# A retention layer fused with a low-rank mixer and an MLP: decay kept inside 64-token chunks instead of on the queries, and the attention steps moved within each tile

## The chip, the core and the metric

The kernel runs on one NeuronCore of a Trainium2 chip. A core has TensorE (PE in the profile, with its weight loads shown apart as PEld), VectorE (DVE), ScalarE (ACT), GpSimd (POOL) and SyncE (SP), each with its own instruction queue, and 16 DMA engines that all queues share. Matrix products land in PSUM; DVE and ACT bring them to SBUF. The metric is the device time of one execution in microseconds (us); lower is better.

## The reference

Eight batches, eight heads, 576 tokens, head width 64, model width 512, MLP width 2048, mixer rank 32:

```python
scores = scale * np.matmul(q, k.transpose(0, 1, 3, 2))
gamma = 1.0 - 2.0 ** (-5.0 - np.arange(H, dtype=np.float32))
Dmat = np.where(rel >= 0, gamma[:, None, None] ** rel[None, :, :], 0.0)   # rel = query - key
ret = scores * Dmat[None, :, :, :]
attn = np.matmul(ret, v)                     # (8, 8, 576, 64), then heads side by side: x (8, 576, 512)
h = xt @ U @ V                               # along the tokens, rank 32
u = x + h.transpose(0, 2, 1)
out = u + np.maximum(u @ w_ch1, 0.0) @ w_ch2
```

There is no softmax, so a query's result is a sum over keys with weights gamma^(query - key). That can be split in chunks of 64 tokens: inside a chunk the scores are computed and masked; everything from earlier chunks comes through one 64x64 state per chunk, the running sum of (key outer value).

## The kernel before

**Tiles and batches.** The MLP works in nine tiles of 512 tokens, which run over the batch borders (a batch has 576). A tile is 32 units on TensorE: units 0 to 15 make the 16 slices of the hidden layer (four accumulating matmuls, then a ReLU on ACT that copies PSUM to SBUF, `y1`), units 16 to 31 make the four output blocks, four units each (then an addition on DVE, `o_sb`, and a store on SP's queue). One unit is four matmuls of 512 columns, some 0.86 us in the trace. Tiles are numbered j = 0 to 8. Batches 0 and 1 and tile 0 are done by `early`, whose order is written out by hand (the string `EARLY`). Then tile j carries the attention of batch j + 1, for j = 1 to 6; tiles 7 and 8 carry none. Where a batch's tokens begin inside a tile, a unit's matmuls are split by columns.

**Steps.** `attention_steps(b, at, gap, at_mixer, at_turn)` lists pieces of a batch's attention with a time in units, and the last loop of the kernel emits, before unit n, every step whose time is at most n. Every engine works through its own instructions in the order emitted. A batch has four head pairs (hp). For each, `att_transposes` at `at[hp]` brings q and k in the layout that TensorE wants, and `visit` at `at[hp] + gap` does the work; a fifth visit at `at[4]` finishes the last pair. For batch 2, q and k are turned on TensorE into PSUM (`psq`, `psk`); ACT copies k (`kvT`) and DVE takes q. From batch 3 on both are turned by DMA transposes (SP's queue) one tile ahead, into `qT_all`/`kT_all` or, every other batch, `qz`/`kvT`.

**One visit.** `visit(b, n)` emits, in this order: the state products of the pair before (`chunk_values`: `xh<-S,q`, 16 matmuls of 64 columns, each waiting for its own slice of `S`); this pair's state terms (`chunk_states`: `pss<-k,v`, 16 to 18 matmuls, and on ACT the copy of the first state to `S`); this pair's scores (`chunk_scores`: `sc<-q,k`, 20 matmuls); the masked scores times v for the pair before (`block_values`: `xh<-v,ret`, 10 matmuls, and on ACT the two copies `x_t<-xh`). Then on DVE: the two masks (`ret<-sc,mask`) and the chain of seven additions `S[g] = pss[g] + S[g-1]`.

**Where the decay is.** gamma^(query - key) is written as gamma^query times gamma^-key over the whole batch. `scale_q_dense` multiplies q by `qsrow` (gamma^token, one row per head) on DVE: 12 head pairs' `qT_all` and 8 pairs' `qz` in place, in bf16, and batch 2's four straight from PSUM. The values are multiplied by gamma^-token times 1/8 (`vscales[2]`): for batch 2 by DVE (`scale_v`, one step per pair, one unit before its transposes), from batch 3 on by POOL, block by block, between its load instructions (`scale_block`). The mask is then 0 or 1 and the same for all heads (`mask64`), and the states only add up.

**Buffers.** PSUM: three banks `mm` shared by the MLP's units and the two `xh` of a visit; three `att` for scores, transposes and the mixer; one double bank for `pss`. The mixer (`mix_middle` at `at_mixer`, five `mix_up` from `at_mixer + 2` half a unit apart, then DMA transposes of `u_t` into `uT_t` from `at_mixer + 3.2`) ends a batch. POOL waits for these transposes before it loads the batch three further on (`wait_for_turns`). In tile 1 the first three units are already done by `early`, and the mixer steps of batch 1 (`late`, at units 14, 20, 24.2, 27, 26 and 29) stand among batch 2's.

Of the kernel before, what the change touches and what calls it, by code (L numbers as in the profile page):

```python
# [8 lines left out]
FP32 = mybir.dt.float32  # L9
BF16 = mybir.dt.bfloat16  # L10
# [53 lines left out]
def kernel(  # L64
# [110 lines left out]
    iota_pc = consts.tile([P, NB], FP32, name="iota_pc")  # L175
    landed = consts.tile([P, NB], BF16, name="landed")
    lnbias = consts.tile([P, 1], FP32, name="lnbias")
    mask64 = consts.tile([P, 2, CH], BF16, name="mask64")
    lngam = consts.tile([P, NHP], FP32, name="lngam")
    qsrow = consts.tile([P, NHP, SP], BF16, name="qsrow")  # L180
    vscales = [consts.tile([P, H, NB], FP32, name=f"vscale{i}") for i in range(NFULL + 1)]
    vexp = consts.tile([P, H, NB], FP32, name="vexp")
    shifted = consts.tile([P, NFULL], FP32, name="shifted")
    masklast = consts.tile([P, 3 * CH], BF16, name="masklast")
    U_sb = [consts.tile([P, NB, P], BF16, name=f"U_sb{i}") for i in range(2)]
    V_sb = [consts.tile([P, SP], BF16, name=f"V_sb{i}") for i in range(2)]
# [55 lines left out]
    def by_head(x):  # L242
        return x.rearrange("p h c -> p c h")[:, :, :, None].to_broadcast([P, NB, H, D])

    vs_b = by_head(vscales[NFULL])

    def scale_v(b, hp):
        v_all = v_sets[b % NSET]
# [60 lines left out]
    def scale_q_runs(b, hp, psq):  # L309

        qT = qz_bufs[hp % 2][:, 0, :]
        c = slice(0, S) if b % 2 == 0 else slice(SP - S, SP)
        dve.tensor_tensor(
            out=by_token(qT[:, c]), in0=psq.rearrange("d i p -> d p i"),
            in1=by_token(qsrow[:, hp, c]), op=ALU.mult,
        )
        return qT

    def att_transposes(b, hp, st):
        if b < NRUNS:  # L320
            psq = turn_runs_by_head(in_runs(q_raw[b % NRUNS]), hp, "psq")
        elif b < NTURN:
            psq = turn_blocks(in_blocks(q_raw[b % NRUNS]), hp, "psq")
        else:
            psq = qT_sets[(b - NTURN) % 2][:, :, hp, :]
        st["qT"] = scale_q_dense(b, hp, psq)
        if b < NTURN:
            psk = turn_blocks(k_sets[b % NSET], hp, "psk")
            st["kT"] = kT_bufs[hp % 2].rearrange("p (c i) -> p c i", c=NB)
            act.copy(out=st["kT"], in_=psk)  # L330
        else:
            st["kT"] = kT_sets[(b - NTURN) % 2][:, :, hp, :]


    def scale_q_dense(b, hp, psq):
        if b >= NTURN:
            dve.tensor_tensor(
                out=psq, in0=psq, in1=qsrow[:, hp, :].rearrange("d (c i) -> d c i", c=NB),
                op=ALU.mult,
            )  # L340
            return [psq[:, g // 2, half(g)] for g in range(NS)]
        qT = scale_q_runs(b, hp, psq)
        return [qT[:, g * CH:(g + 1) * CH] for g in range(NS)]

    def chunk_states(b, hp, st):

        k_all, v_all = (x[b % NSET] for x in (k_sets, v_sets))
        ps = banks["two"].tile([P, 2, 8, CH], FP32, tag="pss", name="pss64")
        gs = places(b)[:-1]
        for g in gs:  # L350
            for hl in range(2):
                h = 2 * hp + hl
                pe.matmul(
                    ps[half(hl), g % 2, g // 2, :], k_all[half(g), g // 2, h, :],
                    v_all[half(g), g // 2, h, :], start=True, stop=True, skip_group_check=True,
                )
        S_sb = work.tile([P, NS - 1, CH], BF16, tag="S_sb", name="S64")
        st["S"] = S_sb
        act.copy(out=S_sb[:, gs[0], :], in_=ps[:, gs[0] % 2, gs[0] // 2, :])

        def add_up():
            for g in gs[1:]:
                dve.tensor_tensor(
                    out=S_sb[:, g, :], in0=ps[:, g % 2, g // 2, :], in1=S_sb[:, g - 1, :],
                    op=ALU.add,
                )

        return add_up

    def chunk_scores(st):  # L370


        sc = [banks["one"].tile([P, 8, CH], FP32, tag="att", name="sc64") for _ in range(2)]
        for g in range(NS):
            for hl in range(2):
                pe.matmul(
                    sc[hl][half(g), g // 2, :], st["kT"][half(hl), g // 2, half(g)],
                    st["qT"][g][half(hl), :], start=True, stop=True,
                    skip_group_check=True,
                )  # L380
        st["ret"] = work.tile([P, 2, NB, P], BF16, tag="ret", name="ret64")

        def mask():
            for hl in range(2):
                dve.tensor_tensor(
                    out=st["ret"][:, hl, :, :].rearrange("p c (i t) -> p c i t", i=2),
                    in0=sc[hl][:, 0:NB, None, :].to_broadcast([P, NB, 2, CH]),
                    in1=mask64[:, None, :, :].to_broadcast([P, NB, 2, CH]), op=ALU.mult,
                )

        return mask
# [13 lines left out]
    def block_values(b, hp, st, xs, x_t):  # L405
        for hl in range(2):
            h = 2 * hp + hl
            for m in range(NB):
                pe.matmul(
                    xs[hl][:, m, :], st["ret"][:, hl, m, :], v_sets[b % NSET][:, m, h, :],  # L410
                    start=False, stop=True, skip_group_check=True,
                )
            act.copy(out=x_t[:, :, h * D:(h + 1) * D], in_=xs[hl][:, 0:NB, :])

    def visit(b, n, sts, x_t):

        if n > 0:
            xs = chunk_values(b, sts[n - 1])
        if n < NHP:
            add_up = chunk_states(b, n, sts[n])  # L420
            mask = chunk_scores(sts[n])
        if n > 0:
            block_values(b, n - 1, sts[n - 1], xs, x_t)
        if n < NHP:
            mask()
            add_up()
# [450 lines left out]
    def exp_of(x):  # L877
        act.activation(out=x, in_=x, func=AF.Exp, bias=lnbias, scale=1.0)
# [66 lines left out]
    for b, x in enumerate(vscales):  # L945
        dve.tensor_tensor(out=x, in0=vexp, in1=places_of, op=ALU.mult)
        if b < NFULL:
            c = ((NB - 1), 0)[b]
            moved = shifted[:, b:b + 1]
            dve.tensor_scalar(  # L950
                out=moved, in0=iota_pc[:, c:c + 1], scalar1=float((-HALF, HALF)[b]),
                scalar2=None, op0=ALU.add,
            )
            dve.tensor_tensor(
                out=x.rearrange("p (g i) c -> p g i c", i=2)[:, :, 1 - b, c],
                in0=vexp.rearrange("p (g i) c -> p g i c", i=2)[:, :, 1 - b, c],
                in1=moved.to_broadcast([P, NHP]), op=ALU.mult,
            )
        if b == 0:
            exp_of(x)  # L960

    dve.memset(U_sb[0], 0.0)
    dve.memset(V_sb[0], 0.0)
# [31 lines left out]
    def between():  # L995

        dve.memset(k_sets[0][HALF:P, NB - 1, :, :], 0.0)
        for i in range(2):
            dve.memset(k_sets[1][half(1 - i), 0, i::2, :], 0.0)
        dve.memset(pairs[0]["u"][HALF:P, NB - 1, :], 0.0)  # L1000
        for x in (k_sets, v_sets):
            dve.memset(x[2][HALF:P, NB - 1, :, :], 0.0)
        dve.memset(q_raw[1][NR:P, :], 0.0)
        for x in at_diag:
            dve.memset(x, 0.0)
        dve.tensor_copy(out=mask64.rearrange("p i t -> p (i t)"), in_=maskbin)
        dve.memset(mask64[0:CH, 1, :], 0.0)

    units1, steps1 = mlp_units(1)
    late = early(mlp_units(0)[1], steps1, between)  # L1010
    for x in (k_sets, v_sets):
        dve.memset(x[3][0:HALF, 0, :, :], 0.0)
    load_batch(3)
# [5 lines left out]
    for j in range(1, NT):  # L1019
        if j == 1:  # L1020
            load_batch(4, range(3))
        steps = []
        if j == 1:
            steps = sorted(
                attention_steps(2, (0, 4.5, 9, 13, 19), 1.5, 20.5, 8) + late,
                key=lambda s: s[:2]
            )
        elif j + 1 < B:
            steps = attention_steps(j + 1, (-1, 3, 7, 11, 17), 1.5, 18.5)
        for n, unit in enumerate(units1 if j == 1 else mlp_units(j)[0]):  # L1030
            while steps and steps[0][0] <= n:
                steps.pop(0)[2]()
            if j > 1 or n >= 3:
                unit()
        for s in steps:
            s[2]()

        if j + 4 < B:
            wait_for_turns(j + 1)
            if j == 1:  # L1040
                load_batch(4, range(3, NB))
            load_batch(j + 4)
# [30 lines left out]
```

## Time and profile before

| | |
|---|---|
| median of 3 runs | 344.21 us (342.31 to 344.47) |
| the profiled execution | 344.57 us |
| its span, first to last instruction | 342.1 us |
| PE busy | 323.0 us, 94% |
| DVE busy | 178.8 us, 52% |
| ACT busy | 143.5 us, 42% |
| POOL busy | 129.2 us, 38% |
| mean granted TensorE clock | 0.995 |

The span is the time between the first and the last instruction; 2.5 us of the execution lie around it. Busy time counts the instructions of an engine; matmuls overlap, and their ends are modelled. In a group or a timeline, "out<-in" names what an instruction writes and reads, "x7" how many are merged, and what stands in brackets is the idle time in front and what ended it. "issue" means that the engine waited for nothing that the profile shows. All instructions carry line 25, a helper through which every operation is made, so groups are told apart by the tiles they write and read.

### The profile page before, as it was taken

What the parts mean: (1) busy time and instruction counts of PE and PEld (TensorE: products, weight loads), DVE (VectorE), ACT (ScalarE), POOL (GpSimd) and SP (SyncE); (2) the same over time, 40 slices, a digit from 0 to 9 for tenths busy, and PEclk for the clock granted to TensorE, in tenths of its full rate; (3) what the DMA queues carried; (4) which work ended last, traced back from release to release, by engine and by line L of the source; (5) the groups of instructions that cost most, each with busy time, mean ns of one, the idle gap of its engine ahead of it and who ended that gap; (6) DMA issues with size and microseconds to landing.
All of it is one profiled execution on the core that took longest, in us unless ns stands there. A gap on an engine that the chain in (4) does not pass through costs nothing.

```text
span 342.1 us, 8895 instructions
## 1 busy us (share of the span) xinstructions
PE 323.0 (94%) x3771; PEld 176.1 (51%) x3800; DVE 178.8 (52%) x432; ACT 143.5 (42%) x304; POOL 129.2 (38%) x166
## 2 busy tenths in 40 slices
PE   7989999979998899898999799999999999999994
PEld 3764455645545664454458654454467544444441
DVE  5866276578775865376437625674477430020011
ACT  7766532557412661076206430474057306504600
POOL 8942784999108991694079420000000000000000
PEclk9999999999999999999999989999999999999999
DMA  8999999999949999999999977640500050011011
GB/s 134 190 207 205 184 201 200 140 147 141 129 108 132 134 163 164 141 161 131 112 133 155 142 65 149 151 59 20 135 34 5 31 140 31 0 63 61 0 61 62
DMA packets 145112, 39.49 MB, mean 115 GB/s; under 512 B 132400, under 2 KB 140336, under 8 KB 145072
## 3 DMA queue, kind: packets, MB, share of 16 engines
q0 software_dynamic: 92848, 17.77, 64.7%
q1 hardware_dynamic: 52224, 21.16, 32.5%
q8 instruction: 29, 0.48, 0.6%
q14 instruction: 11, 0.09, 0.1%
HBM read 37.14 MB, written 9.44 MB: 136 GB/s over the span
## 4 chain that ended last, share of the span: by engine, by line
PE 84%; DVE 6%; DMA 4%; issue 3%; ACT 0%; POOL 0%; DVEq 0%; POOLq 0%
PE ps_y L25 67%; PE ps_b L25 6%; PE xh L25 4%; DMA kv_runs<-in_v_dram 3%; PE sc L25 2%; PE ps_h L25 2%; DVE ret L25 2%; DVE qT_all L25 2%; DMA q_all<-in_q_dram 2%; DVE S L25 1%; DVE v_all L25 1%; DVE qz L25 1%; PE ps_at L25 1%; PE pss L25 1%; PE psk L25 0%
## 5 line engine op out<-in xcount | busy, mean ns | idle before, releaser
L25 ACT ACTIVATE y_t<-ps_y 128x512 bf16<-128x512 f32 x144 | 85.6, 597 | 123.1 <-PE ps_y L25 122.9
L25 PE MATMUL ps_y<-uT_t,w_sb 128*128 128x512 bf16 (+3 forms) x768 | 134.0, 329 | 0.8 <-issue 0.8
L25 PE MATMUL ps_y<-w_sb,y_t 128*128 128x512 bf16 x549 | 129.6, 379 | 2.2 <-issue 1.3
L25 PEld LDWEIGHTS <-w_sb 128*128 128x128 bf16 x768 | 68.9, 99 | 52.4 <-issue 1.1
L25 PEld LDWEIGHTS <-y_t 128*128 128x128 bf16 x576 | 54.9, 98 | 63.4 <-issue 0.3
L25 DVE TENSOR_TENSOR o_sb<-ps_y,u_t 128x512 f32<-128x512 f32 x36 | 24.9, 690 | 107.0 <-PE ps_y L25 107.0
L25 DVE TENSOR_TENSOR ret<-sc,mask 128x640 bf16<-128x640 f32 x48 | 37.3, 819 | 17.4 <-PE sc L25 15.2
L25 DVE TENSOR_TENSOR S<-pss,S 128x64 bf16<-128x64 f32 x168 | 37.4, 223 | 4.9
L25 POOL DMA_DIRECT2D q_all<-in_q_dram x37 | 30.1, 817 | 6.0 <-DMA w_sb<-in_moe_w_ch_dram 3.7
L25 POOL DMA_DIRECT2D k_all<-in_k_dram x30 | 24.4, 816 | 12.4 <-DMA w_sb<-in_moe_w_ch_dram 8.9
L25 DVE TENSOR_TENSOR u_t<-ps_h,x_t 128x512 bf16<-128x512 f32 (+1 forms) x35 | 22.7, 685 | 4.6 <-PE ps_h L25 4.4
L25 ACT CAST x_t<-xh 128x320 bf16<-128x320 f32 x48 | 18.1, 429 | 12.5 <-PE xh L25 11.1
L25 POOL TENSOR_TENSOR v_all<-v_all,vscale 128x512 bf16<-128x512 bf16 (+1 forms) x15 | 16.7, 1116 | 3.9 <-DMA v_all<-in_v_dram 3.9
L25 POOL DMA_DIRECT2D v_all<-in_v_dram x20 | 17.2, 859 | 1.6 <-issue 0.9
L25 POOL COPY landed<-uT_t 128x4 bf16<-128x4 bf16 (+1 forms) x3 | 0.6, 184 | 38.6 <-DMA uT_t<-u_t 38.6
L25 POOL TENSOR_TENSOR kv_runs<-kv_runs,vscale 128x512 bf16<-128x512 bf16 (+1 forms) x10 | 10.7, 1069 | 9.0 <-DMA kv_runs<-in_v_dram 8.8
L25 PEld LDWEIGHTS <-ret 128*128 128x128 bf16 (+1 forms) x320 | 11.6, 98 | 2.9 <-DVE ret L25 0.8
L25 PEld LDWEIGHTS <-kvT 64*64 64x64 bf16 (+3 forms) x360 | 8.4, 103 | 7.0 <-issue 3.9
L25 POOL DMA_DIRECT2D kv_runs<-in_k_dram x14 | 11.3, 804 | 1.3 <-POOLq L1057 0.9
L25 PEld LDWEIGHTS <-k_all 64*64 64x64 bf16 (+2 forms) x456 | 9.2, 109 | 4.5 <-issue 3.1
L25 POOL DMA_DIRECT2D kv_runs<-in_v_dram x14 | 11.1, 793 | 0.2 <-issue 0.2
L25 ACT CAST at_diag<-ps_at 32x128 bf16<-32x128 f32 x24 | 6.2, 257 | 9.6 <-PE ps_at L25 9.4
(104 smaller groups left out, 241.2 us busy)
## 6 DMA issues: line engine op xcount, KB each, us to landing
out_dram<-o_sb SPq DMA_DIRECT2D x36, 256.0 KB, 2.1
w_sb<-in_moe_w_ch_dram POOLq DMA_DIRECT2D x8, 512.0 KB, 11.8
q_all<-in_q_dram POOLq DMA_DIRECT2D x20, 128.0 KB, 7.4
k_all<-in_k_dram POOLq DMA_DIRECT2D x16, 128.0 KB, 9.1
v_all<-in_v_dram POOLq DMA_DIRECT2D x16, 128.0 KB, 9.5
q_all<-in_q_dram POOLq DMA_DIRECT2D x12, 144.0 KB, 6.8
kv_runs<-in_v_dram SPq DMA_DIRECT2D x8, 128.0 KB, 6.3
kv_runs<-in_k_dram POOLq DMA_DIRECT2D x8, 128.0 KB, 7.5
```

Source lines behind the costliest of these rows:

```text
L25: return self._tc.keep_in_program_order(call(*args, **kwargs))
```

## The change

Only batches 2 to 7 are touched. gamma^(query - key) is now counted from the start of each 64-token chunk, in four places, with p the place of a token in its chunk:

- **Queries are not scaled.** From batch 3 on nothing is done to q. For batch 2, `q_by_chunks` copies it from PSUM on ACT.
- **The values** are multiplied by 1/8 times gamma^(64 - p): `vs64`, by the same instructions as before (DVE for batch 2, POOL later), with another table.
- **The masks** take a power and are one per head, in fp32 (`masks`, 8 x 128 x 128, laid over `qsrow`, which `early` has done with). DVE makes them with eight `tensor_scalar` between `early` and tile 1.
- **The copies** `x_t<-xh` on ACT become activations with a per-partition factor (`xs64`).
- **The states** decay by gamma^64 from chunk to chunk: the seven additions become `scalar_tensor_tensor`, S[g] = S[g-1] * keep64 + pss[g], with a per-partition scalar.

Seven tiny set-up instructions come in on DVE and ACT and two go out. The step times change: batch 2's pairs from (0, 4.5, 9, 13, 19) and mixer 20.5 to (3, 7, 11, 15, 20.5) and 22; batches 3 to 7 from (-1, 3, 7, 11, 17) and 18.5 to (-1.5, 2.5, 6.5, 10.5, 16) and 17.8. With the gap of 1.5 the visits of batches 3 to 7 come before units 0, 4, 8, 12 and 16 (were 1, 5, 9, 13, 17), the mixer before unit 18 (was 19). The DMA transposes of the next batch's q and k stay where they are.

```diff
-    vs_b = by_head(vscales[NFULL])
+    vs_b = vs64[:, None, :, None].to_broadcast([P, NB, H, D])
...
-        st["qT"] = scale_q_dense(b, hp, psq)
+        st["qT"] = q_by_chunks(b, hp, psq)
...
-    def scale_q_dense(b, hp, psq):
+    def q_by_chunks(b, hp, psq):
         if b >= NTURN:
-            dve.tensor_tensor(
-                out=psq, in0=psq, in1=qsrow[:, hp, :].rearrange("d (c i) -> d c i", c=NB),
-                op=ALU.mult,
-            )
             return [psq[:, g // 2, half(g)] for g in range(NS)]
-        qT = scale_q_runs(b, hp, psq)
+        qT = qz_bufs[hp % 2][:, 0, :]
+        c = slice(0, S) if b % 2 == 0 else slice(SP - S, SP)
+        act.copy(out=by_token(qT[:, c]), in_=psq.rearrange("d i p -> d p i"))
         return [qT[:, g * CH:(g + 1) * CH] for g in range(NS)]
...
-                dve.tensor_tensor(
-                    out=S_sb[:, g, :], in0=ps[:, g % 2, g // 2, :], in1=S_sb[:, g - 1, :],
-                    op=ALU.add,
+                dve.scalar_tensor_tensor(
+                    out=S_sb[:, g, :], in0=S_sb[:, g - 1, :], scalar=keep64[:, hp:hp + 1],
+                    in1=ps[:, g % 2, g // 2, :], op0=ALU.mult, op1=ALU.add,
                 )
...
-                    in1=mask64[:, None, :, :].to_broadcast([P, NB, 2, CH]), op=ALU.mult,
+                    in1=masks[:, 2 * hp + hl, None, :, :].to_broadcast([P, NB, 2, CH]),
+                    op=ALU.mult,
                 )
...
-            act.copy(out=x_t[:, :, h * D:(h + 1) * D], in_=xs[hl][:, 0:NB, :])
+            act.activation(
+                out=x_t[:, :, h * D:(h + 1) * D], in_=xs[hl][:, 0:NB, :], func=AF.Copy,
+                scale=xs64[:, h:h + 1],
+            )
...
+    for x, i in ((xs64, 0), (vs64, 1)):
+        dve.tensor_tensor(
+            out=x, in0=vexp[:, :, 0], in1=place[:, i:i + 1].to_broadcast([P, H]), op=ALU.mult
+        )
...
+        exp_of(vs64)
+        act.activation(out=xs64, in_=xs64, func=AF.Exp, bias=0.0, scale=-1.0)
+        act.activation(out=keep64, in_=lngam, func=AF.Exp, bias=0.0, scale=float(CH))
...
     late = early(mlp_units(0)[1], steps1, between)
+    for h in range(H):
+        dve.tensor_scalar(
+            out=masks[:, h, :, :], in0=mask64, scalar1=float(gammas[h] ** -CH), scalar2=None,
+            op0=ALU.mult,
+        )
...
-                attention_steps(2, (0, 4.5, 9, 13, 19), 1.5, 20.5, 8) + late,
+                attention_steps(2, (3, 7, 11, 15, 20.5), 1.5, 22, 8) + late,
...
-            steps = attention_steps(j + 1, (-1, 3, 7, 11, 17), 1.5, 18.5)
+            steps = attention_steps(j + 1, (-1.5, 2.5, 6.5, 10.5, 16), 1.5, 17.8)
```

More of the change, by code (lines that the diff above doesn't have):

```diff
@@ L177 @@
     lnbias = consts.tile([P, 1], FP32, name="lnbias")
+    qsrow_ = consts.tile([P, NHP * SP], BF16, name="qsrow")
+    qsrow = qsrow_.rearrange("p (n s) -> p n s", n=NHP)
     mask64 = consts.tile([P, 2, CH], BF16, name="mask64")
+    masks = qsrow_.bitcast(FP32)[:, 0:H * 2 * CH].rearrange("p (h i t) -> p h i t", h=H, i=2)
     lngam = consts.tile([P, NHP], FP32, name="lngam")
-    qsrow = consts.tile([P, NHP, SP], BF16, name="qsrow")
-    vscales = [consts.tile([P, H, NB], FP32, name=f"vscale{i}") for i in range(NFULL + 1)]
+    vscales = [consts.tile([P, H, NB], FP32, name=f"vscale{i}") for i in range(NFULL)]
     vexp = consts.tile([P, H, NB], FP32, name="vexp")
     shifted = consts.tile([P, NFULL], FP32, name="shifted")
+    place = consts.tile([P, 2], FP32, name="place")
+    vs64 = consts.tile([P, H], FP32, name="vs64")
+    xs64 = consts.tile([P, H], FP32, name="xs64")
+    keep64 = consts.tile([P, NHP], FP32, name="keep64")
     masklast = consts.tile([P, 3 * CH], BF16, name="masklast")
@@ L362, in add_up, with chunk_scores @@
             for g in gs[1:]:
-                dve.tensor_tensor(
-                    out=S_sb[:, g, :], in0=ps[:, g % 2, g // 2, :], in1=S_sb[:, g - 1, :],
-                    op=ALU.add,
+                dve.scalar_tensor_tensor(
+                    out=S_sb[:, g, :], in0=S_sb[:, g - 1, :], scalar=keep64[:, hp:hp + 1],
+                    in1=ps[:, g % 2, g // 2, :], op0=ALU.mult, op1=ALU.add,
                 )
         return add_up
-    def chunk_scores(st):
+    def chunk_scores(hp, st):
         sc = [banks["one"].tile([P, 8, CH], FP32, tag="att", name="sc64") for _ in range(2)]
@@ L420, in visit @@
             add_up = chunk_states(b, n, sts[n])
-            mask = chunk_scores(sts[n])
+            mask = chunk_scores(n, sts[n])
         if n > 0:
@@ L960 @@
             exp_of(x)
+    for i in range(2):
+        dve.tensor_scalar(
+            out=place[half(i), 0:1], in0=iota_pc[half(i), 0:1], scalar1=float(-i * CH),
+            scalar2=None, op0=ALU.add,
+        )
+    dve.tensor_scalar(
+        out=place[:, 1:2], in0=place[:, 0:1], scalar1=float(-CH), scalar2=None, op0=ALU.add
+    )
+    for x, i in ((xs64, 0), (vs64, 1)):
+        dve.tensor_tensor(
+            out=x, in0=vexp[:, :, 0], in1=place[:, i:i + 1].to_broadcast([P, H]), op=ALU.mult
+        )
     dve.memset(U_sb[0], 0.0)
@@ L1010 @@
     late = early(mlp_units(0)[1], steps1, between)
+    for h in range(H):
+        dve.tensor_scalar(
+            out=masks[:, h, :, :], in0=mask64, scalar1=float(gammas[h] ** -CH), scalar2=None,
+            op0=ALU.mult,
+        )
     for x in (k_sets, v_sets):
```

## The prediction

> **What bounds the kernel now.** First the page's busy times and the chain that ended last:
>
> ```profile
> PE 323.0 (94%) x3771; PEld 176.1 (51%) x3800; DVE 178.8 (52%) x432; ACT 143.5 (42%) x304; POOL 129.2 (38%) x166
> ...
> PE 84%; DVE 6%; DMA 4%; issue 3%; ACT 0%; POOL 0%; DVEq 0%; POOLq 0%
> ```
>
> TensorE is the bound. The change takes no matmul away, so it can only win what PE waits in tiles 1 to 6. The stretches between the tiles' first matmuls (tiles 1 to 6 in order; PE's busy time is the first after the length) show how much:
>
> ```profile
> 68.72:106.75 38.03, 35.51 (x468) 18.28 (x472) 27.01 (x57) 16.54 (x36) 20.18 (x23) 1.00 1.43 128
> 106.75:142.53 35.78, 33.47 (x463) 19.69 (x463) 22.05 (x50) 14.01 (x32) 25.03 (x30) 1.00 1.59 153
> 142.53:177.78 35.25, 33.26 (x401) 16.22 (x403) 20.54 (x50) 14.07 (x32) 19.74 (x24) 1.00 1.43 136
> 177.78:215.60 37.82, 35.32 (x464) 23.29 (x465) 20.50 (x50) 14.02 (x32) 16.10 (x18) 0.95 1.27 125
> 215.60:249.03 33.43, 33.10 (x400) 16.17 (x402) 19.73 (x50) 14.03 (x32) 0.00 (x0) 1.00 0.42 88
> ```
>
> Idle PE: 2.52, 2.31, 1.99, 2.50, 0.33 us, and 0.32 in tile 6. Next, which wait ends last there: PE's timeline from tile 2 on, with the long idle times in brackets.
>
> ```profile
> 107.45 0.32 PE L25 MATMUL pss<-kv_runs 64*64 64x64 bf16 x16
> 108.71 0.35 PE L25 MATMUL sc<-qT_all,kT_all 64*64 64x64 bf16 x20 [0.95 <-DVE qT_all L25]
> ...
> 112.59 0.32 PE L25 MATMUL xh<-S,qT_all 64*64 64x64 bf16 x16
> ...
> 118.57 0.35 PE L25 MATMUL sc<-qT_all,kT_all 64*64 64x64 bf16 x20 [1.10 <-DVE qT_all L25]
> ...
> 194.53 0.25 PE L25 MATMUL sc<-qT_all,kT_all 64*64 64x64 bf16 x6 [1.90 <-issue]
> ```
>
> The scores wait for the scaling of q. DVE's timeline of tile 2's first visits says why it is late:
>
> ```profile
> 106.68 0.69 DVE L25 TENSOR_TENSOR o_sb<-ps_y,u_t 128x512 f32<-128x512 f32 x1 [2.99 <-PE ps_y L25]
> 107.29 1.37 DVE L25 TENSOR_TENSOR qT_all<-qT_all,qsrow 128x640 bf16<-128x640 bf16 x1
> 109.11 1.55 DVE L25 TENSOR_TENSOR ret<-sc,mask 128x640 bf16<-128x640 f32 x2 [0.45 <-PE sc L25]
> 110.58 1.76 DVE L25 TENSOR_TENSOR S<-pss,S 128x64 bf16<-128x64 f32 x7
> 112.26 0.48 DVE L25 TENSOR_TENSOR qT_all<-qT_all,qsrow 128x640 bf16<-128x640 bf16 x1
> ```
>
> It stands behind the tile's last `o_sb`, or behind the masks and the state chain; and the same instruction takes 0.48 us at 112.26 but 1.37 here and 1.92 at 116.59, each time beside one of POOL's scalings of v (POOL's timeline: 107.20 and 117.07, 1.1 us each). Advanced Engine Details of the Trainium skill (VectorE Performance Modes) says that VectorE's second SBUF port is shared with GpSimd, which fits the 0.48 against 1.37. No term below uses it.
>
> **Part by part.** All against the profiled execution, 344.57 us.
>
> *q is not scaled, batches 3 to 7.* Twenty DVE instructions go (8.9 + 4.6 us busy). Path: tile 2, 0.95 + 1.10 = 2.05; tile 3, 0.87 at 144.41; tile 4, 0.27 at 192.32; and at the start of tiles 4, 5 and 6 the scores come 0.38 us after the states' matmuls where 0.13 is usual, 3 x 0.25 = 0.75. Together 3.94. The other PE waits of these tiles are "issue": 0.85 at 155.15, 1.90 at 194.53. In both PE stops inside a run of alike matmuls, with DVE and ACT done. They are not touched; I keep them.
>
> *What is late next: the state chain.* `xh<-S` of the next visit waits for each slice of S. In tile 2 the chain ends at 110.58 + 1.76 = 112.34 and PE gets there at 112.59: 0.25 us to spare at the first visit, 117.02 against 116.67 = 0.35 at the second, about 0.5 at the next two. Now the first visit moves ahead of unit 0. Its scores end about 0.35 us after the tile's last matmul, but DVE has `o_sb` first (next start 0.61 later), then the masks (1.47) and the chain (1.76): 3.84 us after that matmul. PE has 0.24 of issue up to the end of the scores, then four units, 3.56: 3.80. The spare time is gone: 0.05 us of waiting x 5 tiles = 0.25.
>
> *The chain's new instruction.* The trace has no three-operand DVE instruction with a pointer scalar. Nearest row: the addition it replaces, same sizes, same PSUM operand, 223 ns (7 in 1.76 us). Far row: on ACT, a pointer factor takes 128x640 from 692 ns (`kvT<-psk`) to 816 (`qsrow<-iota_col,lngam`), +124. I see no reason for less than 223. I take 223; 124 ns more is the upper end and a rival.
>
> *Masks in fp32, one per head.* `ret` reads PSUM and a mask, 819 ns for 640 columns; `v_all<-kv_runs,vscale` with two fp32 tensors in SBUF takes 825 for the same 640. Nothing, to at most 0.3 us in all 48.
>
> *Factor in the `x_t` copies.* 429 ns, plus between 0 and 124: two per visit, up to 0.25 us. ACT is 14.0 of 33.4 us busy in tile 5, and the bank that the second copy frees is wanted two units (1.73 us) later. Hidden; nothing. ScalarE: Activation LUTs of the Trainium skill (What ACT_TABLE_LOAD costs) puts a pointer operand at about 93 ns, the trace at 124 with another function; if DVE's pointer cost the same 93, the chain would be 0.65 us longer and the sum about 347 (an estimate from that page and the spare times above).
>
> *Steps half a unit sooner.* The last visit now stands right behind unit 15, and the first output block needs the bank of that unit's ReLU: 0.60 us on ACT against 0.56 of visit, some 0.1 x 5 = 0.5. Mixer, `mix_up`, and the transposes of `u_t` (3.2 us to landing) come a unit earlier; on SP's queue they pass one store, whose data come later anyway, and POOL's next loads start up to 0.86 us sooner. Nothing waits for either in tiles 3 to 7: no gain, no loss.
>
> *Tile 1.* Now PE waits 0.58 (`kvT`), 1.33 (`v_all`) and 0.35 (`qz`), since batch 2's first visits come before there are units to cover them: three units later all 2.26 go. New there: the eight masks on DVE (128x128 fp32 `tensor_scalar`, 312 ns in `iota_col`: up to 2.5 us) ahead of the first `v_all`, which would be ready between 70.9 and 71.9 where PE wants it at 71.1: 0.4. Later `v_all` beside POOL (0.75 to 1.78 us), with 0.36 to spare: 0.3. ACT takes q (0.65 us) besides `kvT`, 4.7 of a visit's 5.2 us: 0.3 by late ReLUs. Three `mix_up` at unit 25 and three at 26 for three banks, with DVE at 0.61 each: 0.3. Sum 1.3. The batch's last turn comes at unit 26 to 27 and lands 3.2 us later, a unit or less ahead of tile 2: nothing, 1 us if DVE is late. Setting-up: 0.6 us on DVE before 8.60, where it idles 1.72, and 0.95 on ACT in tile 0, which idles 0.27 per unit: nothing.
>
> **Sum.** Gone: 3.94 + 2.26 = 6.20. New: 0.25 + 0.5 + 1.3 = 2.05. 344.57 - 4.15 = **340.4 us**, 1.1% under the median of 344.21, which the profiled execution is 0.36 above.
>
> **Rivals.**
>
> 1. *The half clock stays away too.* Right after the 1.90 us wait the clock granted falls to half for 3.4 us, which costs some 1.7:
>
> ```profile
> 193.00:195.00 2.00, 0.47 (x16) 0.43 (x17) 0.19 (x1) 0.00 (x0) 0.00 (x0) 1.00 1.60 97
> ...
> 196.00:197.00 1.00, 1.00 (x7) 0.67 (x6) 0.93 (x4) 0.60 (x1) 0.38 (x1) 0.50 2.15 156
> ```
>
> Without the 0.27 before it, or with DMA falling otherwise, PE may not idle enough. For: one of the three runs before is 2 us shorter. Against: the 1.90 has its own cause. 340.4 - 1.7 = 338.7; with both "issue" waits gone (2.75) 336.0. TensorE: Matmul & The Clock Gate of the Trainium skill (HAM oscillation) asks for idle gaps of over about 3.4 us; here 1.90 was enough in a window, so the trace disagrees with that rule.
>
> 2. *The gain is handed on.* If the "issue" waits end by something that keeps its own pace (a DMA that loads run against), PE only reaches them sooner and waits longer: of the 3.94, tile 3's and 4's 1.6 go, and the start of tile 2 loses up to 1: 340.4 + 2.6 = 343.0, no change. For: the waits stand only in tiles 3 and 4, where DMA is busy at 1.3 to 1.4, none in 5 and 6 at 0.4 and less. Against: tile 2's 2.05 have no such wait behind them.
>
> 3. *The chain becomes the bound: slower.* With a pointer scalar at +124 ns it is 0.87 us longer; the four waits of a tile are 0.05 + 0.87, and 0.87 less 0.35, 0.5, 0.5: 2.18, x 5 = 10.9, less the 0.25 counted, and about 1 in tile 1: 340.4 + 11.6 = 352. It eats the whole gain at about +80 ns and makes the kernel 1% slower at +100. For: ACT's rows. Against: DVE's fixed part is near 155 ns in every two-operand row (223 for 64 columns, 819 for 640), whatever the operands.
>
> 4. *The scaling of q was only where the wait ended:* then `kT_all`'s transposes or the banks end it next. Against: they landed a tile earlier. It would be 344; small.
>
> **Numbers.** A measurement here tells about 1% from no change. Forecast 340.4 (339 to 342.5): 0.45. Rival 1, 336 to 339: 0.20. Rivals 2 and 4, 342.5 to 345: 0.19. Rival 3, up to 352: 0.16. Below 340.8 (1% faster) lie a good half of the first, all of the second: 0.48; within 1%, the rest of the first, the third and the mild end of rival 3: 0.38; slower 0.14. Range 336.0 to 347, which leaves out the worst of rival 3 and little else.
>
> **What would show it.** `sc` in tiles 2 to 6 with no idle time; `S<-pss,S` near 223 ns; `xh<-S` without waits named DVE beyond 0.1; tile 2 near 34 us and tile 1 near 37. Wrong if `S` takes 300 ns, if "issue" grows in tiles 2 to 4, or if tile 2 starts with a wait for `uT_t`.

## The result, and the profile after

| | before | changed |
|---|---|---|
| median of 20 runs each | 342.78 us (340.91 to 346.53) | 340.38 us (337.89 to 343.29) |
| the profiled execution | 344.57 us, span 342.1 | 340.07 us, span 338.1 |

The ratio is 0.9929, with a 95% interval of 0.9902 to 0.9956: 0.7% faster. A ratio, here and below, leaves out executions more than 1.5% above the fastest of the same kernel; a median counts all. The forecast was 340.4 us, but as 4.15 us off a profiled execution of 344.57. Between the two profiled executions 4.5 us went, between the medians 2.4: the profiled one stood 1.8 above the median that 20 runs give. Of the 4.5 us, 3.7 lie in tiles 1 to 6, 0.3 behind the last `o_sb` and 0.5 outside the span, and for these last 0.8 the prediction had put down nothing. The experiments below show a part of what makes single runs differ. Another part was not tested: the stretch before tile 1, up to the last `o_sb` of tile 0, takes 63.9 us in both of these profiles and 63.2 to 68.9 in the fourteen of this study.

The page of the changed kernel, on the lines that answer to those of before (in the groups: mean ns of one after the comma):

```profile
PE 324.6 (96%) x3775; PEld 176.6 (52%) x3800; DVE 173.3 (51%) x420; ACT 150.0 (44%) x310; POOL 129.1 (38%) x166
...
q8 instruction: 29, 0.48, 0.6%
...
PE 63%; DVE 7%; issue 1%
...
L25 DVE SCALAR_TENSOR_TENSOR S<-S,keep,pss 128x64 bf16<-128x64 bf16 x168 | 47.0, 280 | 5.1
L25 DVE TENSOR_TENSOR ret<-sc,qsrow 128x640 bf16<-128x640 f32 x48 | 37.3, 819 | 15.4 <-PE sc L25 13.8
...
L25 ACT ACTIVATE x_t<-xh,xs 128x320 bf16<-128x320 f32 x48 | 22.7, 524 | 8.6 <-PE xh L25 7.6
```

The masks cost what they did (819 ns, fp32 or not). The copies with a factor went from 429 to 524 ns, the chain's instruction from 223 to 280. The same stretches as before, tile 1 to tile 5, cut at each tile's first matmul, which is now a visit's:

```profile
68.64:105.37 36.73, 35.67 (x463) 18.07 (x466) 25.66 (x58) 18.73 (x40) 19.12 (x22) 1.00 1.26 127
105.37:139.20 33.83, 33.60 (x464) 19.80 (x465) 19.57 (x45) 14.91 (x32) 25.46 (x30) 1.00 1.73 163
139.20:173.50 34.30, 33.66 (x401) 16.15 (x403) 19.56 (x45) 14.90 (x32) 20.26 (x25) 1.00 1.55 141
173.50:211.20 37.70, 35.41 (x464) 23.35 (x465) 19.57 (x45) 14.90 (x32) 15.37 (x17) 0.95 1.30 124
211.20:244.90 33.70, 33.45 (x400) 16.22 (x401) 19.56 (x45) 14.90 (x32) 0.00 (x0) 1.00 0.42 87
```

Tile 2 lost 1.95 us, tile 3 0.95, tile 1 about 1.1. Tile 4 is as long as it was, and tile 5 is 0.27 longer. PE's timeline shows the new wait of tile 2 and the old one of tile 4:

```profile
105.37 0.32 PE L25 MATMUL pss<-kv_runs 64*64 64x64 bf16 x16
105.52 0.33 PE L25 MATMUL sc<-qT_all,kT_all 64*64 64x64 bf16 x20
105.78 3.67 PE L25 MATMUL ps_y<-uT_t,w_sb 128*128 128x128 bf16 x32
109.38 0.61 PE L25 MATMUL xh<-S,qT_all 64*64 64x64 bf16 x16
...
189.46 0.42 PE L25 MATMUL xh<-v_all,ret 128*128 128x64 bf16 x9 [2.06 <-issue]
```

The scores follow the state terms at once. But 16 `xh<-S` matmuls now take 0.61 us at 109.38, where 0.32 is usual: they wait one by one for the slices of S. DVE says why:

```profile
105.48 0.69 DVE L25 TENSOR_TENSOR o_sb<-ps_y,u_t 128x512 f32<-128x512 f32 x1 [2.99 <-PE ps_y L25]
106.09 1.55 DVE L25 TENSOR_TENSOR ret<-sc,qsrow 128x640 bf16<-128x640 f32 x2
107.55 2.17 DVE L25 SCALAR_TENSOR_TENSOR S<-S,keep,pss 128x64 bf16<-128x64 bf16 x7
```

The order is the forecast one, `o_sb`, masks, chain; the chain takes 2.17 us where 1.76 was put down, and ends at 109.72, 0.34 after PE came for it. The prediction's sign for this, no wait named DVE beyond 0.1, would have missed it: the waits in front of single `xh<-S` matmuls are 0.1 at most, and the loss is in the length of the group.

### The profile page after: what moved, and what is told of

Read it like the earlier page. It is cut to its first block, busy times and chain, and to the rows that moved or that the text cites. A ratio compares the mean times of both kernels' runs of the same rounds, so it can differ in the third digit from the quotient of the medians.

```text
span 338.1 us, 8895 instructions
## 1 busy us (share of the span) xinstructions
PE 324.6 (96%) x3775; PEld 176.6 (52%) x3800; DVE 173.3 (51%) x420; ACT 150.0 (44%) x310; POOL 129.1 (38%) x166
## 4 chain that ended last, share of the span: by engine, by line
PE 63%; DVE 7%; issue 1%
PE ps_y L25 55%; PE xh L25 4%; DVE S L25 3%; DVE ret L25 2%; PE ps_h L25 2%; DVE o_sb L25 1%; DVE u_t L25 1%; PE sc L25 1%; PE ps_at L25 1%; PE pss L25 1%; PE ps_ut L25 0%
## 5 line engine op out<-in xcount | busy, mean ns | idle before, releaser
L25 DVE SCALAR_TENSOR_TENSOR S<-S,keep,pss 128x64 bf16<-128x64 bf16 x168 | 47.0, 280 | 5.1
L25 DVE TENSOR_TENSOR ret<-sc,qsrow 128x640 bf16<-128x640 f32 x48 | 37.3, 819 | 15.4 <-PE sc L25 13.8
L25 ACT CAST S<-pss 128x64 bf16<-128x64 f32 x24 | 5.0, 210 | 54.0 <-issue 50.0
L25 ACT ACTIVATE x_t<-xh,xs 128x320 bf16<-128x320 f32 x48 | 22.7, 524 | 8.6 <-PE xh L25 7.6
L25 POOL TENSOR_TENSOR v_all<-v_all,vs 128x512 bf16<-128x512 bf16 (+1 forms) x15 | 16.0, 1065 | 4.9 <-DMA v_all<-in_v_dram 4.8
L25 POOL TENSOR_TENSOR kv_runs<-kv_runs,vs 128x512 bf16<-128x512 bf16 (+1 forms) x10 | 11.0, 1102 | 10.1 <-DMA kv_runs<-in_v_dram 9.9
```

What stands on the lines that cost most here:

```text
L25: return self._tc.keep_in_program_order(call(*args, **kwargs))
```

## The experiments

My theory: the wait for the scaled q was the loss before; what the change gives back is the longer chain behind `o_sb`; the "issue" waits are a thing of their own. The rival: the moved steps win, and the new decay hardly matters. Each time is a median, with the kernel before run in turn on the same chip; the rounds ran on different chips, so kernels of different rounds are compared by their ratios. Single runs spread over 2.6 to 10 us, so small differences are read from tiles instead, one execution of each kernel. One table for all, from each run's profile: the time from the start of a tile's last `o_sb` on DVE to that of the next tile's.

| kernel | tile 2 | tile 3 | tile 4 | tile 5 | tile 6 | median, us | ratio to before (95%) |
|---|---|---|---|---|---|---|---|
| before | 35.78 | 35.25 | 37.82 | 33.43 | 33.58 | | |
| changed | 33.85 | 34.27 | 37.71 | 33.70 | 33.82 | 340.38 | 0.9929 (0.9902 to 0.9956) |
| e1 old steps | 33.79 | 33.37 | 36.12 | 33.36 | 33.48 | 341.86 | 0.9991 (0.9954 to 1.0029) |
| e2 steps only | 35.53 | 35.49 | 38.67 | 34.50 | 34.66 | 346.30 | 1.0122 (1.0055 to 1.0188) |
| e3 no scaling of q | 33.36 | 34.08 | 35.64 | 33.17 | 33.33 | 340.11 | 0.9898 (0.9855 to 0.9941) |
| e4 plain chain | 33.56 | 33.83 | 37.33 | 33.38 | 33.54 | 339.53 | 0.9927 (0.9888 to 0.9966) |
| e5 constant factor | 33.56 | 33.61 | 37.92 | 33.38 | 33.54 | 339.29 | 0.9871 (0.9819 to 0.9923) |
| e6 chain first | 33.56 | 33.74 | 36.23 | 33.38 | 33.54 | 342.43 | 0.9959 (0.9915 to 1.0003) |
| e7 five units | 33.36 | 34.89 | 38.52 | 33.18 | 33.34 | 340.10 | 0.9896 (0.9838 to 0.9955) |
| e8 shift 64 | 33.85 | 33.72 | 34.26 | 33.71 | 33.82 | 338.57 | 0.9830 (0.9764 to 0.9896) |
| e9 five units, masks, shift 64 | 33.36 | 33.18 | 33.82 | 33.18 | 33.34 | 337.16 | 0.9794 (0.9749 to 0.9840) |
| e10 five units, masks | 33.36 | 34.40 | 37.62 | 33.18 | 33.34 | 341.36 | 0.9937 (0.9903 to 0.9971) |
| e11 shift 128 | 34.09 | 34.28 | 34.07 | 33.70 | 33.82 | 338.47 | 0.9849 (0.9794 to 0.9904) |
| e12 before, shift 64 | 33.89 | 34.56 | 34.05 | 33.43 | 33.58 | 341.15 | 0.9925 (0.9886 to 0.9964) |

Tiles 5 and 6, where no loads run, agree to some 0.02 us between kernels whose work there is alike: there a few hundredths can be read. Tiles 3 and 4 vary with the "issue" waits.

### The two halves of the change: e1 and e2

e1, the changed kernel with the old step times:

```diff
-                attention_steps(2, (3, 7, 11, 15, 20.5), 1.5, 22, 8) + late,
+                attention_steps(2, (0, 4.5, 9, 13, 19), 1.5, 20.5, 8) + late,
-            steps = attention_steps(j + 1, (-1.5, 2.5, 6.5, 10.5, 16), 1.5, 17.8)
+            steps = attention_steps(j + 1, (-1, 3, 7, 11, 17), 1.5, 18.5)
```

> The changed kernel with the step times of the kernel before; medians so far 342.8 before, 340.4 changed. Theory (q off DVE wins, the longer chain of S loses): tile 1 loses its shift again, about +1.0; in tiles 2 to 6 the first visit stands behind unit 0 again, so that o_sb no longer holds the chain up: of the 0.4 us wait per tile about half stays, and the last visit's bank wait goes, -1.5. About 340 (339 to 341). Rival (the moved steps are what wins): 342.5 or more.

e2 is the reverse, the kernel before with the new step times.

> The kernel before with the step times of the changed one; q is still scaled on DVE. Theory: tile 1 gains 1 us, but in tiles 2 to 6 the first scores now stand ahead of unit 0 and wait for o_sb and the scaling, 1.1 to 2 us a tile where it was 0.25 to 0.95: slower, 344 to 347. Rival (the moved steps win by themselves): 341 or less.

e2 came out as the theory has it, 1.2% slower. The moved steps are no gain for the old arithmetic; its scores wait at the start of every tile, as in this timeline of PE in tile 5:

```profile
218.62 0.32 PE L25 MATMUL pss<-v_all,k_all 64*64 64x64 bf16 x16
219.87 0.35 PE L25 MATMUL sc<-qz,kvT 64*64 64x64 bf16 x20 [0.93 <-DVE qz L25]
```

e1 came out 1.9 us above its number, 0.9 above its range, and is no faster than before. Its tiles are what I expected: tiles 5 and 6 at 33.36 and 33.48, 0.34 better than with the moved steps. So there the move costs 0.3 us a tile; in tile 2 an "issue" wait of 0.43 hides it. In the profiled execution the loss is in tile 1, on DVE and then on PE:

```profile
69.93 3.49 DVE L25 TENSOR_SCALAR qsrow<-mask 128x128 f32<-128x128 bf16 x8
73.42 0.55 DVE L25 MEMSET kv_runs<- 64x256 uint32 x2
73.89 0.75 DVE L25 TENSOR_TENSOR v_all<-v_all,vs 128x640 bf16<-128x640 bf16 x1
```

```profile
74.69 0.43 PE L25 MATMUL pss<-v_all,k_all 64*64 64x64 bf16 x16 [2.55 <-DVE v_all L25]
```

The eight masks, 1.7 us busy in the changed kernel's profile, take 3.49 here, and the first scaling of v stands behind them. With the old times nothing covers that, and the half clock came with it (74.2 to 77.6). So the rival is right for tile 1: there the three units' delay covers what the new arithmetic puts in. How much it covers differs from run to run: with masks of 1.7 us the wait here would be some 0.7 (an estimate, 2.55 less the 1.8 that they took longer).

### What the scaling of q was worth: e3

```diff
         if b >= NTURN:
-            dve.tensor_tensor(
-                out=psq, in0=psq, in1=qsrow[:, hp, :].rearrange("d (c i) -> d c i", c=NB),
-                op=ALU.mult,
-            )
             return [psq[:, g // 2, half(g)] for g in range(NS)]
```

> The kernel before without the scaling of q for batches 3 to 7 (their output then lacks that factor), all else alike. Theory: the 3.9 us of PE waits in tiles 2 to 6 that end with this scaling go and nothing takes their place, 339 (338 to 340). Rival (something else ends these waits next, a transpose or a bank): 342 or more.

1.0% off, and nothing in its place: 3.4 us between the medians (2.0 to 5.0 by the ratio's interval) where 3.9 was expected. Tile 2 gives 2.42, tiles 5 and 6 0.25 each. That 0.25 is the pause between state terms and scores which the prediction read off the timeline.

### The chain: e4, e5 and e6

e4 puts the plain addition back; e5 keeps the three-operand instruction but with a constant:

```diff
-                    out=S_sb[:, g, :], in0=S_sb[:, g - 1, :], scalar=keep64[:, hp:hp + 1],
+                    out=S_sb[:, g, :], in0=S_sb[:, g - 1, :], scalar=float(gammas[2 * hp] ** CH),
```

> The changed kernel with the plain addition in the chain of S instead of the three-operand instruction (the states then do not decay from chunk to chunk). Theory: 7 x 57 ns = 0.4 us less ahead of the second visit of each tile, the wait of 0.4 there nearly gone, -2 us: 338.4. Rival (the chain is only where the wait ended, o_sb and the masks hold the visit anyway): 340.

> The changed kernel with a constant of the program in place of the pointer scalar in the chain of S (one factor for both heads of a pair, so the decay is not exact). If the pointer costs the 57 ns, S takes 223 ns and the time is that of the plain chain, 338.4; if it is the three-operand instruction itself, S stays at 280 ns and the time at 340.4.

e5's group of S:

```profile
L25 DVE SCALAR_TENSOR_TENSOR S<-S,pss 128x64 bf16<-128x64 bf16 x168 | 36.8, 219 | 4.9
```

219 ns with a constant, 280 with a pointer: the pointer scalar costs 61 ns an instruction, the third operand nothing. Both kernels bring tile 5 from 33.70 to 33.38, so the pointer costs 0.32 us a tile, 1.6 in five; I had expected 0.4. Both medians lie about 1 us under the changed kernel's, but the ratios do not tell them apart from it: e4's is the same, and e5's interval overlaps.

e6 makes the chain before the masks:

```diff
-            mask()
-            add_up()
+            add_up()
+            mask()
```

> The changed kernel with the chain of S ahead of the two masks on DVE in every visit. Theory: the next visit needs S 0.55 us before it needs ret, so the chain's 0.4 us wait goes and ret is just in time: -2 us, 338.4. Rival: ret becomes late by as much, 340.4.

Tiles 2, 5 and 6 are those of e4 and e5, to the hundredth: with S ahead the pointer's price is hidden, and `ret` is in time. But the whole kernel is not faster: by the ratios (0.9959 and 0.9929) it is not told apart from the changed kernel. Its profiled execution, the longest of its twelve, shows a loss in tile 1. Batch 2 is turned on TensorE into the same three banks that the masks free, and these now come free later:

```profile
80.29 0.44 PE L25 MATMUL psk<-ident,k_all 128*128 128x128 bf16 x5 [0.90 <-DVE ret L25]
86.20 0.44 PE L25 MATMUL psk<-ident,k_all 128*128 128x128 bf16 x5 [0.70 <-DVE ret L25]
```

With two smaller waits of that kind this takes 2.0 us in tile 1, more than the 1.6 won; the changed kernel's profile has no such wait. That it is the same in the other eleven executions is not shown. Both theories had looked only from tile 2 on.

### Room for the chain: e7

```diff
-            steps = attention_steps(j + 1, (-1.5, 2.5, 6.5, 10.5, 16), 1.5, 17.8)
+            steps = attention_steps(j + 1, (-1.5, 3, 7, 11, 17), 1.5, 18.5)
```

> The changed kernel with five units instead of four between the first two visits of tiles 2 to 6: visits before units 0, 5, 9, 13 and 17, mixer before 19. Theory: the chain has a unit (0.86 us) more where it was 0.4 us late, and the last visit's bank is free: -2.5 us, 337.9. Rival (the wait only moves to a later visit): 340.

Tiles 2, 5 and 6 fall to 33.36, 33.18 and 33.34, the values of e3, which has no scaling of q and the short chain: nothing of the new decay is left on the path. Against e6 that is another 0.20, the bank that the last visit left to the first output block. The median gained only 0.3 us on the changed kernel's (ratios 0.9896 and 0.9929, not told apart). In its profile, the longest of its six executions, tiles 3 and 4 came out 1.4 us longer than the changed kernel's, by "issue" waits, which there takes back more than half of what the steps give.

### The "issue" waits: e8, e11 and e12

The page counts 29 packets of the queue called instruction, 0.48 MB: 16,384 bytes each. PE ran 7575 recorded instructions; 0.48 MB over these is some 64 bytes, so a packet is 256 instructions. In the profiles of e3, e5, e7 and e10, which have all or nearly all of PE's 7620 records, every "issue" wait over 0.4 us stands at PE instruction 448, 704, 2240, 4032 or 5056, counted from the start: each 192 beyond a multiple of 256. And each ends 1.2 to 1.6 us after such a packet has come, but one, the longest (e7, at 5056), 2.2: in the changed kernel the packet ran from 187.19 to 188.12 and PE went on at 189.46; before, 191.90 to 193.19 and 194.53. To test it, PE gets more instructions at the very start:

```diff
+                if b == 8:
+                    for _ in range(40):
+                        pe.matmul(
+                            ps[:, 0, 0:100], warm, warm[:, 0:100], start=True, stop=True,
+                        )
+                    return
                 for _ in range(b):
                     pe.matmul(
                         ps, warm, warm[:, None, :].to_broadcast([P, 4, P]),
```

(e11: 72 of 56 columns.)

> The changed kernel with 64 more PE instructions at the very start (the first eight warm-up matmuls of 512 columns cut into 40 of 100). Theory (the waits named issue are PE waiting for its next 256 instructions): the 2.06 us wait of tile 4 and the 0.4 us wait of tile 3 stand 64 PE instructions earlier in the tile, whatever matmuls these are, at sizes of their own; the time within 2 us of 340.4. Rival (they hang on the matmuls where they stand, or on a transfer that these use): they stay in the fourth visit of tile 4, among the matmuls of ret.

> The changed kernel with 128 more PE instructions at the start (72 warm-up matmuls of 56 columns). Theory: every wait named issue of some length stands at a PE instruction whose number, counted from the start, is 192 beyond a multiple of 256, so 128 PE instructions earlier in the tile than in the changed kernel; their sizes change, the time stays within 2.5 us of 340.4. Rival: the waits stand at the same matmuls as in the changed kernel.

In e8 the waits of tiles 3 and 4 are gone: no "issue" wait over 0.15 us is left there, so the expected ones 64 instructions earlier in the tile did not come. One of 0.95 stands in tile 1, at instruction 2496, again 192 beyond a multiple of 256 and in other matmuls. In e11 two short ones stand at 4288 and 5312, the next such places of the count (128 PE instructions later in the tile than in the changed kernel; those 128 earlier show none), now among the matmuls of `ret` in the fourth visit of tile 3 and the last of tile 4:

```profile
154.17 0.38 PE L25 MATMUL xh<-v_all,ret 128*128 128x64 bf16 x7 [0.40 <-issue]
192.66 0.25 PE L25 MATMUL xh<-v_all,ret 128*128 128x64 bf16 x3 [0.28 <-issue]
```

The plainest case stands before tile 1, at instruction 704. In eight of the ten unshifted profiles PE waits there among the scores; with 64 more instructions it waits at the same count, but among the transposes of q. First the changed kernel, then e8:

```profile
21.92 0.46 PE L25 MATMUL sc<-qz,kvT 64*128 64x128 bf16 x6 [1.10 <-issue]
...
20.11 0.28 PE L25 MATMUL ps_b<-ident,q_all 96*64 96x96 bf16 x4 [1.70 <-issue]
```

So where they come, the waits go by the count, not by the matmuls: PE waits for its own next block of instructions. Shown is the place in the count and the packet ahead of the end. In the changed kernel's tile 4 the packet itself starts only as PE runs dry (187.19, and PE stops at 187.40), so it is its start that is late; that the loads, on the same 16 DMA engines, make it late is argued, from tiles 5 and 6, which have no loads and no such wait. In neither run did the clock fall to half in tile 4. Both are near 338.5, by the ratios 1.0 and 0.8% below the changed kernel (e8's interval lies apart from its, e11's just touches it), by nothing but 64 or 128 more instructions. The shift by 64 also has a price: at 704 e8, e9 and e12 wait 1.7 to 2.2 us, where the unshifted profiles wait 1.1 at most, and the half clock follows (21.7 to 25.1 in e8).

e12 gives the kernel before the same 64.

> The kernel before with the 64 more PE instructions at the start, and nothing of the change. Theory: its waits of 1.04 us in tile 3 and 1.90 in tile 4 (and the half clock after the latter) shrink as they did in the changed kernel, 1.5 to 2.5 us: 341.5 (340 to 342.5), the profile's tile 4 at 36 or less where it was 37.8; the waits for the scaled q in tiles 2, 3 and 4 stay. Rival (the shift only helps the changed kernel): 343.5.

341.15: the shift helps it as much, 0.8%. So it has nothing to do with the change, and in the comparison of the two kernels it cancels: 0.983 against 0.9925, about 1.0%. Its tile 2 is 33.89 where it was 35.78, though q is still scaled: the four scalings of q took 0.48, 0.81, 0.48 and 0.48 us there, where before they took 1.37, 0.48, 1.92 and 0.48. Two of them lie beside POOL's scalings of v here too, but cost DVE less. With the first, DVE kept its 0.48 and POOL's took 1.40, where 1.10 is usual:

```profile
112.64 0.48 DVE L25 TENSOR_TENSOR qT_all<-qT_all,qsrow 128x640 bf16<-128x640 bf16 x1
...
112.63 1.40 POOL L25 TENSOR_TENSOR v_all<-v_all,vscale 128x512 bf16<-128x512 bf16 x1
```

In tiles 3 and 4 the slow scalings are there as before (1.25 and 1.22 us, before 1.29 and 1.25). The waits named `qz` or `qT_all` behind tile 1 sum to 1.25 us instead of 3.2. The wait for q was thus no fixed price either.

### Together: e9 and e10

e10 has e7's steps, and the masks of a pair are made in that pair's own step, behind its scaling of v; e9 has the shift by 64 besides.

```diff
                 steps.append((at[hp] - 1, 4, lambda hp=hp: scale_v(b, hp)))
+                steps.append((at[hp] - 1, 4.5, lambda hp=hp: pair_masks(hp)))
...
     late = early(mlp_units(0)[1], steps1, between)
-    for h in range(H):
-        dve.tensor_scalar(
-            out=masks[:, h, :, :], in0=mask64, scalar1=float(gammas[h] ** -CH), scalar2=None,
-            op0=ALU.mult,
-        )
```

> The same without the 64 more PE instructions. Theory: 340.4 - 2.5 - 1 = 337 (335.5 to 339), with the waits in tiles 3 and 4 at the PE instructions where the changed kernel had them. Rival: no better than five units alone (340.1).

> The changed kernel with five units between the first two visits, each pair's two masks made in the pair's own step behind its scaling of v (not all eight ahead of tile 1), and 64 more PE instructions at the start. Theory: the first gives -2.5 us (tiles 2, 5 and 6 at 33.2 to 33.4 as with five units alone), the second takes the wait for v_all at the start of tile 1 (0.86 to 2.55 in three profiles), -1, the third moves the waits for PE instructions to a place where tiles 3 and 4 had none: 335 (333 to 337). Rival (the shift was luck): like the same without the shift.

e9 is the fastest kernel of this study: 337.16 us, 2.1% under before; all six of its runs (335.46 to 338.07) are faster than all 17 of before beside it. It is 2 us above the expected 335. e10 missed by 4: both long waits were back at 4032 and 5056, with the half clock behind the second.

```profile
153.07 2.98 PE L25 MATMUL ps_y<-uT_t,w_sb 128*128 128x512 bf16 x13 [1.05 <-issue]
192.33 0.27 PE L25 MATMUL sc<-qT_all,kT_all 64*64 64x64 bf16 x7 [2.48 <-issue]
```

The wait for `v_all` at the first visit of tile 1 is gone in both. e10 differs from e7 by the masks' place alone, and the two are not told apart (ratios 0.9937 and 0.9896). e9 differs from e10 by the shift alone and is 1.4% faster (0.9794 and 0.9937, the intervals apart): most of e9's gain over the changed kernel is the shift.

## Why the prediction was right, point by point

- **The bound and the removed waits.** Right: `sc` waits for q nowhere. In tile 2 the waits for q were worth 2.42 (e3), more than the 2.05 read from the rows, and 0.52 of new ones came, which leaves the 1.9 measured. The 3.4 between medians (e3) fit the sum of 3.94, within a wide interval.
- **The order of what is late next.** Right: `o_sb`, masks, chain, then `xh<-S` of the second visit, and only there; the other visits did not wait for it (in tile 2, for one, a later visit's chain ends at 114.00 and its `xh` begins at 114.10).
- **The chain's instruction: mis-sized.** I took the row of the two-operand addition, 223 ns; it is 280, between the two ends and nearer to the far one's rise (124, on ACT) than I gave it weight for. The term "0.05 x 5 = 0.25" was 0.32 x 5 = 1.6 us. The rule on ACT's pointer operand (ScalarE: Activation LUTs of the Trainium skill, What ACT_TABLE_LOAD costs), about 93 ns, is borne out on ACT by `x_t`, 524 less 429 = 95 ns; on DVE the pointer takes 61. In `x_t` the copy also became an activation, so the 95 is not the pointer's alone. Rival 3 needed 80 and did not decide.
- **The last visit's bank.** Named rightly, at 0.1 us a tile; e7 against e6 shows 0.20, 1.0 in five tiles in place of 0.5. Tile 5 is then the sum of the three: -0.25 for q, +0.32 for the chain, +0.20 for the bank, +0.27 as measured.
- **Tile 1.** -0.96 predicted, -1.1 found, in part by luck: in the changed kernel's profile the masks took 1.7 us and the first `v_all`, put down as 0.4 late, was in time, while in e1 and e8 they took 3.5 and it was 2.55 and 0.86 late. A range would have been the better term.
- **The "issue" waits, kept.** Right in the sum (2.75 before, 2.46 after at the two places). The clock's fall in tile 4 stayed too, so rival 1 did not come in that execution. It came in e8 and e11, where the wait itself is gone, and in e1, e3 and e6, where the wait stayed. Nor did rival 2, the gain handed on: tile 4 got only 0.1 shorter, but there 0.52 us of waits for q went, 0.52 came with the chain and the bank, and its "issue" wait was hardly another (2.06 after 1.90). In its sum rival 2 counts 1.6 us of waits for q in tiles 3 and 4; the rows give 0.87, 0.27 and 0.25, which is 1.39.
- **The size of the gain.** The 4.15 us are near the 4.5 of this pair of profiles, though only 3.7 of these lie in the tiles that the sum is about, and 1.7 too many for the medians. Two things in the sum were too favourable. The chain and the bank were put down 1.85 us too small (0.25 for 1.6 and 0.5 for 1.0), which alone is as much as the 1.7. And the waits for q were summed in one execution, in which two of DVE's scalings in tile 2 were slow beside POOL's; e12's execution has the same code with 1.25 us of such waits in place of 3.2. How much of the 1.7 is due to each is not shown. The forecast met the median by luck, because two errors offset: a base 1.8 above the median of before, and a gain 1.7 above the one between medians.

## What to carry to other kernels

Before a sum of waits is taken as the gain, ask of each wait whether it must recur, and at what size: a collision between two engines' free-running streams, or a late block of instructions, is one draw, and the median of many runs need not have it. When an operation leaves the critical engine's path, size the chain that stands behind it with the new instruction's real price, pointer operands included, and give the first consumer one unit more room rather than one less. Where single runs spread by 1%, compare stages that nothing disturbs; here two tiles without loads told 0.2 us apart when the medians could not.

## What the runs showed of the hardware that was not expected

- A pointer scalar on a DVE `scalar_tensor_tensor` of 64 columns costs 61 ns (280 against 219 with a constant); three operands cost no more than two (219 against 223).
- PE's instructions arrive in blocks of 256 (packets of 16,384 bytes, worked out above), and PE waited 0.3 to 3.3 us at places 192 beyond a multiple of 256 in the count; it went on 1.2 to 1.7 us after the packet had come, and twice 2.2. Moving the count by 64 or 128 changed the time by 0.8 to 1.4%. Why 192 is open.
- In ten profiles PE idled 1.9 to 3.3 us at the "issue" wait of tile 4, in a stretch of small matmuls. In seven of them 3.4 us at half clock followed (190.0 to 193.4 in the changed kernel) and the tile took 37.3 to 38.7 us; in e1, e3 and e6, with waits of 2.1 to 2.5, the clock stayed and it took 35.6 to 36.2. Before tile 1 the half clock followed "issue" waits of 1.3 to 2.2 us (e7 to e10 and e12) and none of 0.4 to 1.1. What decides in tile 4 is open.
- Eight `tensor_scalar` of 128x128, the same instructions in eight kernels, took 1.7 us in one profile, 1.9 to 2.4 in four and 3.5 to 3.6 in three. POOL scales v in this stretch, but in e1 its scaling covers only 1.1 of the 3.5 us; what decides is open.
